# Seven products in place of eight for the output projection of a bilinear feed-forward block, with tokens split by parity

## The chip, the cores and the metric

The kernel runs on one core of a Trainium2 chip. The metric is device time in microseconds (us), the median of several executions; a change counts as faster or slower from 2% on. Ratios are the mean time of one kernel's fast runs over that of the other's fast runs in the same rounds, so they differ a little from the ratio of the medians quoted.

Engines in the profile's lines: PE is TensorE's matmul, PEld its weight load, DVE VectorE, ACT ScalarE, POOL GpSimd, SP SyncE.

## The reference

```python
# attention: batch 8, heads 8, seq 576, head_dim 64; 4 heads local (32 back), 4 strided (every 32nd)
scores = q @ k.T / 8, masked;  attn = softmax(scores);  x = attn @ v      # -> x: 4608 tokens x 512
a = x @ w_a                       # 512 -> 1536
b = x @ w_b                       # 512 -> 1536
out = (a * b) @ w_out             # 1536 -> 512
```

The change concerns the last line alone.

## The kernel before: the parts concerned

Tokens go in nine tiles of 512. A tile has twelve *blocks* of d_ff: eight matmuls of 512 columns give 128 rows of a and of b in PSUM (call the twelve together the *wide part*). ScalarE copies a to SBUF, and VectorE multiplies it by b into `pf`. Four groups of twelve matmuls then make the output (the *output stretch*). A tile is 16 slots; between slots, score units (S) and value units (V) of the next batch's attention are put in.

```python
def ffn_ab(t, f, mid, ab=None):
    ...
    ab = [psum4["mm"].tile([128, TTOK], F32, tag="mm", name="mm") for _ in range(2)]   # 3 banks in all
    ...                                              # 4 + 4 matmuls of 512 columns
    nc.scalar.copy(a_sb, ab[0])
    nc.vector.tensor_mul(pf[:, f, :], a_sb, ab[1])   # 512 bf16, one plain run

def ffn_y(t, j, mid):
    ...
    for f in range(FD):                              # 12
        nc.tensor.matmul(y, lhsT=pf[:, f, 128 * j:128 * (j + 1)], rhs=wo_sb[:, f, c0:c0 + n], ...)
    ...                                              # copy to SBUF, store

def step_VT(b, u):                                   # value unit: 6 or 8 matmuls, then
    ...
    nc.scalar.activation(r, sums, ACT.Ln)
    nc.scalar.activation(r, r, ACT.Exp, scale=-1.0)
    ...                                              # two VectorE multiplications that wait for these
```

In the traces VectorE takes its instructions in program order (the prediction shows it idle for 2.61 us with ready work behind).

The softmax here doesn't subtract the row's maximum and nothing guards it: scores larger than these inputs give would overflow.

## Time and profile before

| | before |
|---|---|
| time, median (lowest to highest) | 343.75 us (342.25 to 344.11) |
| TensorE busy | 98% |
| VectorE, ScalarE busy | 60%, 60% |
| wide part of tile 4, its output stretch | 24.05 us, 11.40 us |
| wide part of tile 7 (no attention), its output stretch | 20.72 us, 10.36 us |

The last two rows are stretches from the first matmul of one part to the first of the next. The lines behind them are in the prediction.

### The profile page before, as it was taken

How to read it: one execution, taken by the hardware profiler on the slowest of the kernel's cores; microseconds unless marked ns; L12 is line 12 of the kernel's file. 1: busy time of each engine (PE TensorE's matmuls, PEld its weight loads, DVE VectorE, ACT ScalarE, POOL GpSimd, SP SyncE). 2: the span in 40 equal slices, each digit the busy share in tenths (PEclk: the TensorE clock that was granted, in tenths of full speed). 3: DMA queues.
4: the chain of work that ended last, by engine and by line, in shares of the span. 5: the costliest groups of instructions: out<-in, count | busy, mean ns of one | idle time of the engine just before them, and what ended most of it. 6: DMA issues, size and time to landing. Idle time of an engine off the chain costs nothing.

```text
span 341.5 us, 6887 instructions
## 1 busy us (share of the span) xinstructions
PE 333.1 (98%) x2520; PEld 173.7 (51%) x2520; DVE 205.1 (60%) x400; ACT 203.9 (60%) x331; POOL 140.4 (41%) x247
## 2 busy tenths in 40 slices
PE   8999999989989999999999999999999999999995
PEld 6754555445545555555555555555555444444444
DVE  6866657758759766876578846885666333303331
ACT  5754865368767765876587657775688533223311
POOL 8945539898537434653465346633000000000000
PEclk9999999999999999999999999999999999999999
DMA  9999999997999599969997989888220110021002
GB/s 160 154 203 197 202 176 172 179 154 89 129 200 101 90 99 185 99 110 91 165 104 133 77 168 96 132 80 145 76 59 2 61 63 0 0 92 34 0 31 94
DMA packets 102242, 37.56 MB, mean 110 GB/s; under 512 B 77632, under 2 KB 97728, under 8 KB 102208
## 3 DMA queue, kind: packets, MB, share of 16 engines
q0 software_dynamic: 87760, 19.58, 63.7%
q1 hardware_dynamic: 14304, 17.47, 16.2%
q8 instruction: 20, 0.33, 0.4%
q14 instruction: 14, 0.11, 0.1%
q10 hardware_dynamic: 144, 0.07, 0.1%
HBM read 39.71 MB, written 9.44 MB: 144 GB/s over the span
## 4 chain that ended last, share of the span: by engine, by line
PE 70%; DMA 17%; SPq 3%; DVE 3%; ACT 3%; POOL 2%; issue 2%; DVEq 0%; ACTq 0%
PE mm L518 41%; PE mm L546 20%; DMA vl<-in_v_dram 4%; PE o L438 3%; PE st L340 3%; DMA k<-in_k_dram 3%; DMA wa_sb<-in_moe_w_a_dram 3%; SPq L302 2%; DMA qz01l<-tq 2%; PE misc L153 2%; DMA out_dram<-y_sb 1%; DMA qz01s<-tq 1%; ACT xr L447 1%; DMA qz11s<-tq 1%; DVE tq L283 1%
## 5 line engine op out<-in xcount | busy, mean ns | idle before, releaser
L518 PE MATMUL mm<-xT,wb_sb 128*128 128x512 bf16 x424 | 110.1, 379 | 0.3
L518 PE MATMUL mm<-xT,wa_sb 128*128 128x512 bf16 x424 | 110.2, 379 | 0.1
L536 DVE TENSOR_TENSOR pf<-a_sb,mm 128x512 bf16<-128x512 f32 x106 | 71.9, 678 | 48.3 <-PE mm L518 25.5
L546 PE MATMUL mm<-wo_sb,pf 128*128 128x512 bf16 (+2 forms) x456 | 99.6, 368 | 0.1
L535 ACT COPY a_sb<-mm 128x512 f32<-128x512 f32 x106 | 62.1, 586 | 45.4 <-PE mm L518 43.0
L518 PEld LDWEIGHTS <-wb_sb 128*128 128x128 bf16 x432 | 41.7, 98 | 49.5 <-issue 1.3
L546 PEld LDWEIGHTS <-pf 128*128 128x128 bf16 x456 | 41.5, 98 | 42.3 <-issue 0.4
L518 PEld LDWEIGHTS <-wa_sb 128*128 128x128 bf16 x432 | 38.1, 98 | 34.2 <-issue 0.2
L552 ACT COPY y_sb<-mm 128x512 f32<-128x512 f32 (+2 forms) x35 | 20.0, 571 | 46.6 <-PE mm L546 38.6
L348 ACT ACTIVATE p<-st 128x576 bf16<-128x576 f32 (+1 forms) x64 | 41.7, 651 | 8.8 <-PE st L340 8.2
L447 ACT ACTIVATE xr<-o 64x576 f32<-64x576 f32 x48 | 31.1, 647 | 23.5 <-PE o L438 23.3
L454 DVE TENSOR_TENSOR xT<-o,xr 64x288 bf16<-64x288 f32 x48 | 21.6, 450 | 33.1 <-ACT xr L448 32.8
L448 ACT ACTIVATE xr<-xr 64x576 f32<-64x576 f32 x48 | 32.8, 682 | 1.5
L452 DVE TENSOR_TENSOR xT<-o,xr 64x288 bf16<-64x288 f32 x48 | 21.6, 450 | 16.9 <-ACT xr L448 16.4
L678 POOL CAST pace<-pf 1x1 f32<-1x1 bf16 x51 | 11.6, 227 | 41.5 <-DVE pf L536 41.3
L358 DVE TENSOR_TENSOR p<-p,mask_l 128x576 int16<-128x576 int16 x32 | 14.6, 455 | 17.1 <-ACT p L348 17.1
L218 POOL DMA_DIRECT2D vs<-in_v_dram x24 | 19.6, 817 | 9.9 <-issue 9.9
L194 POOL DMA_DIRECT2D kl<-in_k_dram x24 | 16.0, 666 | 6.7 <-issue 5.0
L194 POOL DMA_DIRECT2D ql<-in_q_dram x24 | 16.0, 666 | 6.6 <-DMA wo_sb<-in_moe_w_out_dram 3.8
L185 POOL DMA_DIRECT2D natk<-in_k_dram x24 | 14.6, 610 | 3.6 <-issue 3.0
L185 POOL DMA_DIRECT2D natq<-in_q_dram x24 | 14.6, 609 | 0.0
L678 POOL COPY pace<-y_sb 1x1 f32<-1x1 f32 x22 | 4.2, 189 | 24.2 <-ACT y_sb L552 24.2
(116 smaller groups left out, 316.2 us busy)
## 6 DMA issues: line engine op xcount, KB each, us to landing
out_dram<-y_sb SPq DMA_DIRECT2D x35, 256.0 KB, 2.4
vl<-in_v_dram POOLq DMA_DIRECT2D x7, 384.0 KB, 6.6
kl<-in_k_dram POOLq DMA_DIRECT2D x24, 72.0 KB, 2.8
ql<-in_q_dram POOLq DMA_DIRECT2D x24, 72.0 KB, 3.3
vs<-in_v_dram POOLq DMA_DIRECT2D x24, 72.0 KB, 3.6
wo_sb<-in_moe_w_out_dram POOLq DMA_DIRECT2D x4, 384.0 KB, 11.9
natk<-in_k_dram POOLq DMA_DIRECT2D x20, 72.0 KB, 3.3
natq<-in_q_dram POOLq DMA_DIRECT2D x20, 72.0 KB, 3.3
```

The costliest lines, as they stand in the source:

```text
L185: nc.gpsimd.dma_start(out=t[32 * h:32 * h + n], in_=bass.AP(tensor=src.tensor, offset=(b * H + HL + h) * S * D, ap=[[RS * D, n], [YS * RS ...
L194: nc.gpsimd.dma_start(out=t[32 * h:32 * h + 32], in_=src[b, h].rearrange("(i y) d -> y i d", y=32))
L348: nc.scalar.activation(p[:M, :, :W], st[:M, :, :W], ACT.Exp, scale=scale)
L447: nc.scalar.activation(r, sums, ACT.Ln)
L448: nc.scalar.activation(r, r, ACT.Exp, scale=-1.0)
L452: nc.vector.tensor_mul(dst[:, W * half:W * (half + 1)], o[:64, j, :W], r[:, j])
L454: nc.vector.tensor_mul(dst.rearrange("d (p r) -> d p r", r=RS)[:, :, G * half:G * (half + 1)], o[:64, j, :W].rearrange("d (g p) -> d p g", ...
L518: nc.tensor.matmul(ps_, lhsT=w[:, kk, 128 * f:128 * (f + 1)], rhs=xT[:, kk, TTOK * t:TTOK * (t + 1)], start=(kk == first), stop=(kk == last))
L535: nc.scalar.copy(a_sb, ab[0])
L536: nc.vector.tensor_mul(pf[:, f, :], a_sb, ab[1])
L546: nc.tensor.matmul(y, lhsT=pf[:, f, 128 * j:128 * (j + 1)], rhs=wo_sb[:, f, c0:c0 + n], start=(f == 0), stop=(f == FD - 1))
L552: (nc.scalar.copy if act else nc.vector.tensor_copy)(y_sb, y)
```

## The change

Strassen's scheme makes a product of 2 x 2 blocks from seven block products. The blocks here are: tokens even and odd, d_ff blocks even and odd, output columns left and right. Seven products of half the columns replace eight, so TensorE should gain an eighth of the output product in tiles 1 to 8. For it, sums of the blocks of `pf` (VectorE and GpSimd) and of `w_out` (VectorE, once) are needed, and the products are combined afterwards. To make room in SBUF, x is kept for four batches in a ring, and the sums of `pf` share a buffer with the loads of the first batches.

```diff
+    XR = 4
-    xT = const.tile([128, KD, n_tok], BF16)
+    xT = const.tile([128, KD, XR * S], BF16)          # a tile across the ring's end: two matmuls for one
 ...
+        if t in FAST_Y:                                # tiles 1 to 8
+            halves = lambda x: x.rearrange("p (m i) -> p m i", i=2)
+            nc.vector.tensor_mul(pf[:, f, :].rearrange("p (i m) -> p m i", i=2), halves(a_sb), halves(ab[1]))
+        else:
             nc.vector.tensor_mul(pf[:, f, :], a_sb, ab[1])
 ...
+    def fast_s(t, n, gs):                              # sums of blocks: n = 0 on GpSimd, 1 and 2 on VectorE
 ...
+            if k == "3":   v["a"] = copy of bank a     # ScalarE
+            elif k == "4": v["w"] = bank b + v["a"]    # VectorE
+            elif k == "1": v["e"] = bank c + v["w"]    # VectorE
+            elif k == "2": v["y21"] = copy of bank b; v["h"] = v["w"] - v["y21"]   # ScalarE, GpSimd
+            elif k == "5": v["y12"] = copy of bank a; v["g"] = v["e"] - v["y12"]   # ScalarE, GpSimd
+            elif k == "6": v["y22"] = bank c + v["h"]  # VectorE
+            else:          v["y11"] = v["g"] - bank d  # VectorE
 ...
+        # products 3, 4, 1 open banks a, b, c; 2, 5, 6 are added onto b, a, c; 7 opens d
+        for k, b, lhs, rhs in (("3", "a", ...), ("4", "b", ...), ("1", "c", ...),
+                               ("2", "b", ...), ("5", "a", ...), ("6", "c", ...), ("7", "d", ...)):
+            ...                                        # 2 x 6 matmuls of 256 columns each
```

(The code of the combining is shortened to one line per product.) The banks also rotate over four in place of three from tile 1 on. The two lines with `halves` put even tokens into the first half of the row and odd ones into the second; in the order in which the program lists the elements, element 0 goes to place 0, element 1 to place 256, element 2 to place 1, and so on. The output rows are stored by parity accordingly.

More of the change, by code (lines that the diff above doesn't have):

```diff
@@ L26 @@
 WCH = (0, 2, 5, 8, 10, 12)
+FAST_Y = (1, 2, 3, 4, 5, 6, 7, 8)
 @with_exitstack
@@ L160, with fast_w @@
     wo_sb = wp.tile([128, FD, d_model], BF16)
+    FG = FD // 2
+    HT = TTOK // 2
+    HN = d_model // 2
+    wf = wp.tile([128, 5, FG, HN], BF16, name="wf")
+    wov = wo_sb.rearrange("p (g e) (j n) -> p e j g n", e=2, j=2)
+    def fast_w(n, gs):
+        a, b, op = ((wov[:, 0, 1], wov[:, 1, 1], ALU.subtract), (wov[:, 1, 0], wov[:, 0, 0], ALU.subtract),
+                    (wov[:, 0, 0], wov[:, 1, 1], ALU.add), (wov[:, 0, 0], wov[:, 0, 1], ALU.add),
+                    (wov[:, 1, 0], wov[:, 1, 1], ALU.add))[n]
+        nc.vector.tensor_tensor(wf[:, n, gs], a[:, gs], b[:, gs], op=op)
     tl = {}
@@ L168 @@
     nats = {}
+    shared = {}
     def load_qk(b, strided, heads=range(HL), names="kq"):
@@ L174, in load_qk @@
                 n, R, h0 = (NP, RS, HL) if strided else (96, RL, 0)
-                if (b, nm, strided) not in nats:
-                    nats[b, nm, strided] = nat.tile([n, HL, R, D], BF16, tag=f"{nm}{R}", name=f"{nm}{R}", bufs=1)
-                t = nats[b, nm, strided]
+                w0 = {"k6": 0, "q6": 1536, "k8": 3072, "q8": 5120}[f"{nm}{R}"]
+                if b not in shared:
+                    shared[b] = nat.tile([128, 5 * FD * TTOK // 4], BF16, tag="shared", name="shared")
+                t = nats[b, nm, strided] = shared[b][:n, w0:w0 + HL * R * D].rearrange("p (h r d) -> p h r d", r=R, d=D)
                 hs = slice(heads[0], heads[-1] + 1)
@@ L449, in step_VT @@
         for j in range(2):
-            dst = xT[64 * j:64 * j + 64, c, S * b:S * (b + 1)]
+            dst = xT[64 * j:64 * j + 64, c, S * (b % XR):S * (b % XR + 1)]
             if c < 2:
@@ L469, in X_e @@
         tv = tp.rearrange("d (g p) -> d g p", p=n)
-        dst = xT[:, c, S * b:S * (b + 1)]
+        dst = xT[:, c, S * (b % XR):S * (b % XR + 1)]
         if c >= 2:
@@ L511, with mm_bank @@
     pfs = {}
+    used = [0]
+    def mm_bank(shape):
+        nm = "tp" if used[0] % 4 == 3 and used[0] >= 0 else "mm"
+        used[0] += 1
+        return psum4[nm].tile(shape, F32, tag=nm, name="mm")
     def ab_mm(t, f, ab, kks, mid=None, first=0, last=KD - 1):
+        n = min(TTOK, XR * S - TTOK * t % (XR * S))
+        cuts = [(0, n)] + ([(n, TTOK - n)] if n < TTOK else [])
         for w, ps_ in zip((wa_sb, wb_sb), ab):
@@ L517, in ab_mm @@
             for kk in kks:
-                nc.tensor.matmul(ps_, lhsT=w[:, kk, 128 * f:128 * (f + 1)], rhs=xT[:, kk, TTOK * t:TTOK * (t + 1)],
-                                 start=(kk == first), stop=(kk == last))
+                for c0, n in cuts:
+                    x0 = (TTOK * t + c0) % (XR * S)
+                    nc.tensor.matmul(ps_[:, c0:c0 + n], lhsT=w[:, kk, 128 * f:128 * (f + 1)], rhs=xT[:, kk, x0:x0 + n],
+                                     start=(kk == first and c0 == 0), stop=(kk == last and c0 == cuts[-1][0]))
     def ffn_ab(t, f, mid, ab=None):
@@ L525, in ffn_ab @@
         if ab is None:
-            ab = [psum4["mm"].tile([128, TTOK], F32, tag="mm", name="mm") for _ in range(2)]
+            ab = [mm_bank([128, TTOK]) for _ in range(2)]
             if f == 0:
@@ L535, in ffn_ab @@
         nc.scalar.copy(a_sb, ab[0])
-        nc.vector.tensor_mul(pf[:, f, :], a_sb, ab[1])
-        return pf[:1, f, :1]
+        if t in FAST_Y:
+            halves = lambda x: x.rearrange("p (m i) -> p m i", i=2)
+            nc.vector.tensor_mul(pf[:, f, :].rearrange("p (i m) -> p m i", i=2), halves(a_sb), halves(ab[1]))
+        else:
+            nc.vector.tensor_mul(pf[:, f, :], a_sb, ab[1])
+        return pf[:1, f, :1]
+    pss = {}
+    def fast_s(t, n, gs):
+        if t not in pss:
+            pss[t] = nat.tile([128, 5 * FD * TTOK // 4], BF16, tag="shared", name="ps").rearrange("p (g m) -> p g m", g=FG)
+        s = pss[t][:, gs]
+        x = pfs[t].rearrange("p (g e) (i m) -> p g e i m", e=2, i=2)[:, gs]
+        if n == 0:
+            nc.gpsimd.tensor_tensor(s[:, :, 0:HT], x[:, :, 0, 0], x[:, :, 1, 1], op=ALU.add)
+        elif n == 1:
+            nc.vector.tensor_tensor(s[:, :, HT:3 * HT].rearrange("p g (i m) -> p g i m", i=2), x[:, :, 0], x[:, :, 1], op=ALU.add)
+        else:
+            nc.vector.tensor_tensor(s[:, :, 3 * HT:].rearrange("p g (e m) -> p g e m", e=2), x[:, :, :, 1], x[:, :, :, 0],
+                                    op=ALU.subtract)
@@ new lines, with y_plan, f32t, store @@
+    yst = {}
+    def y_plan(t):
+        pf, s = pfs[t], pss[t]
+        full = lambda e, i: (lambda g, q: pf[:, 2 * g + e, HT * i + 128 * q:HT * i + 128 * (q + 1)])
+        summed = lambda n: (lambda g, q: s[:, g, HT * n + 128 * q:HT * n + 128 * (q + 1)])
+        wsum = lambda n: (lambda g: wf[:, n, g])
+        wfull = lambda e, j: (lambda g: wov[:, e, j, g])
+        bank = {}
+        v = {}
+        def f32t(nm, bufs):
+            return fsb.tile([128, 2, HN], F32, tag=nm, name=nm, bufs=bufs)
+        def store(y, i, j, q=slice(0, 2), n=slice(0, HN)):
+            rows = out[TTOK * t:TTOK * (t + 1), HN * j:HN * (j + 1)].rearrange("(q p i) c -> p i q c", q=2, i=2)
+            nc.sync.dma_start(out=rows[:, i, q, n], in_=y[:, q, n])
+        def post(k):
+            if k == "3":
+                v["a"] = f32t("ya", 1)
+                nc.scalar.copy(v["a"], bank["a"])
+            elif k == "4":
+                v["w"] = v["a"]
+                nc.vector.tensor_tensor(v["w"], bank["b"], v["a"], op=ALU.add)
+            elif k == "1":
+                v["e"] = f32t("ye", 1)
+                nc.vector.tensor_tensor(v["e"], bank["c"], v["w"], op=ALU.add)
+            elif k == "2":
+                v["y21"] = f32t("y_sb", 4)
+                nc.scalar.copy(v["y21"], bank["b"])
+                store(v["y21"], 1, 0)
+                v["h"] = v["w"]
+                nc.gpsimd.tensor_tensor(v["h"], v["w"], v["y21"], op=ALU.subtract)
+            elif k == "5":
+                v["y12"] = f32t("y_sb", 4)
+                nc.scalar.copy(v["y12"], bank["a"])
+                store(v["y12"], 0, 1)
+                v["g"] = v["e"]
+                nc.gpsimd.tensor_tensor(v["g"], v["e"], v["y12"], op=ALU.subtract)
+            elif k == "6":
+                v["y22"] = f32t("y_sb", 4)
+                nc.vector.tensor_tensor(v["y22"], bank["c"], v["h"], op=ALU.add)
+                store(v["y22"], 1, 1)
+            else:
+                last(slice(0, 2), slice(0, HN))
+        def last(q, n):
+            if "y11" not in v:
+                v["y11"] = f32t("y_sb", 4)
+            nc.vector.tensor_tensor(v["y11"][:, q, n], v["g"][:, q, n], bank["d"][:, q, n], op=ALU.subtract)
+            store(v["y11"], 0, 0, q, n)
+        for k, b, lhs, rhs in (("3", "a", full(0, 0), wsum(0)), ("4", "b", full(1, 1), wsum(1)), ("1", "c", summed(0), wsum(2)),
+                               ("2", "b", summed(2), wfull(0, 0)), ("5", "a", summed(1), wfull(1, 1)),
+                               ("6", "c", summed(3), wsum(3)), ("7", "d", summed(4), wsum(4))):
+            new = b not in bank
+            if new:
+                bank[b] = mm_bank([128, 2, HN])
+            tail = k == "7" and t == NT - 1
+            for q in range(2):
+                for n in ((slice(0, 128), slice(128, 256)) if tail and q == 1 else (slice(0, HN),)):
+                    for g in range(FG):
+                        nc.tensor.matmul(bank[b][:, q, n], lhsT=lhs(g, q), rhs=rhs(g)[:, n],
+                                         start=new and q == 0 and g == 0, stop=g == FG - 1, skip_group_check=True)
+                        if g == FG - 1:
+                            if tail:
+                                last(slice(q, q + 1), n)
+                            elif q == 1:
+                                post(k)
+                        yield v
@@ L539, in ffn_y, with ffn_ys @@
+    def ffn_ys(t, j, mid):
+        if j == 0:
+            yst[t] = y_plan(t)
+        n = 21 + (6 if (t, j) == (NT - 1, 3) else 0)
+        for i in range(n):
+            v = next(yst[t])
+            if i == n // 2:
+                mid()
+        if j == 3:
+            for _ in yst[t]:
+                pass
+        return v[("a", "e", "y12", "y11")[j]][:1, 0, :1]
     def ffn_y(t, j, mid):
@@ L543, in ffn_y @@
         for z, n in enumerate((256, 128, 128) if (t, j) == (NT - 1, 3) else (d_model,)):
-            y = psum4["mm"].tile([128, n], F32, tag="mm", name="mm")
+            y = mm_bank([128, n])
             for f in range(FD):
@@ L549, in ffn_y @@
                     mid()
-            y_sb = fsb.tile([128, n], F32, tag="y_sb", name="y_sb", bufs=3)
+            y_sb = fsb.tile([128, n], F32, tag="y_sb", name="y_sb", bufs=4)
             act = t < NT - 1 or (j + z) % 2 == 1
@@ L631 @@
         for t in range(NT):
-            slots += [(ffn_ab, t, f) for f in range(FD)] + [(ffn_y, t, j) for j in range(4)]
+            slots += [(ffn_ab, t, f) for f in range(FD)] + [(ffn_ys if t in FAST_Y else ffn_y, t, j) for j in range(4)]
         steps = {}
@@ L672 @@
             do(i, fill_v, t)
+        for n in range(5):
+            for z in range(2):
+                do(17 + 2 * n + z, fast_w, n, slice(3 * z, 3 * z + 3))
+        for t in FAST_Y:
+            for n, at_ in ((0, (3, 7, 11)), (1, (4, 8, 11)), (2, (5, 9, 11))):
+                for z in range(3):
+                    do(16 * t + at_[z], fast_s, t, n, slice(2 * z, 2 * z + 2))
         for i, (fn, t, j) in enumerate(slots):
+            if i == 0:
+                used[0] = -1000 * 3
+            elif i == 16:
+                used[0] = 0
             mid = lambda: take(i - 0.5)
-            done = fn(t, j, mid) if fn is ffn_y else fn(t, j, mid, first.get(j) if t == 0 else None)
+            done = fn(t, j, mid) if fn is not ffn_ab else fn(t, j, mid, first.get(j) if t == 0 else None)
             if i > 13 and i in at:
```

## The prediction

> **What bounds the kernel now.** I read the page's busy shares first, then sums by stretch, then the timelines of TensorE and VectorE around one output product.
>
> ```profile
> span 341.5 us, 6887 instructions
> PE 333.1 (98%) x2520; PEld 173.7 (51%) x2520; DVE 205.1 (60%) x400; ACT 203.9 (60%) x331; POOL 140.4 (41%) x247
> ```
>
> TensorE is busy for 98%. A busy row alone could be padding, since the page says that ends are modelled, so I looked at starts. The timeline of the last tile has groups of four matmuls of 512 columns:
>
> ```profile
> 317.97 1.03 PE L518 MATMUL mm<-xT,wb_sb 128*128 128x512 bf16 x4
> 318.84 1.03 PE L518 MATMUL mm<-xT,wa_sb 128*128 128x512 bf16 x4
> 319.70 1.03 PE L518 MATMUL mm<-xT,wb_sb 128*128 128x512 bf16 x4
> ```
>
> A group starts every 0.865 us: 216 ns a matmul, not the 379 ns of the rows. TensorE really streams. Sums by stretch, columns as on the page (stretch, length, then PE, PEld, DVE, ACT, POOL busy, clock, DMA):
>
> ```profile
> 170.07:194.12 24.05, 24.02 (x185) 12.52 (x183) 18.22 (x34) 19.09 (x31) 13.00 (x26) 1.00 0.96 105
> 194.12:205.52 11.40, 11.40 (x83) 5.72 (x80) 6.58 (x13) 5.82 (x11) 5.01 (x10) 1.00 0.84 148
> 296.39:306.75 10.36, 10.36 (x49) 4.70 (x48) 0.69 (x1) 1.76 (x3) 0.00 (x0) 1.00 0.20 76
> 335.25:336.56 1.31, 1.31 (x14) 1.17 (x13) 0.69 (x1) 0.00 (x0) 0.00 (x0) 1.00 0.05 13
> ```
>
> The first two are tile 4: its two wide products, then its output product with two value and two score units in it. The third is tile 7's output product alone, 48 matmuls: 10.36/48 = 216 ns. The fourth runs from the first of the twelve 256-column matmuls of the tail to the matmul after them: 1.31/12 = 109 ns. So half the columns cost half the time, and the separate weight load of each, although its row says 98 ns, stays hidden. The only long TensorE waits are some 3 us around 68 and 94 us, for transposed q landing. **TensorE's stream is the bound, in every tile.**
>
> VectorE is at 18.22 of 24.05 us in the wide part, and does its work strictly in program order. Its timeline at tile 4's output product, which starts at 194.12 (I call that T):
>
> ```profile
> 194.67 0.69 DVE L536 TENSOR_TENSOR pf<-a_sb,mm 128x512 bf16<-128x512 f32 x1
> 195.28 0.45 DVE L358 TENSOR_TENSOR p<-p,mask_s 72x576 int16<-72x576 int16 x1
> 195.65 0.70 DVE L288 STREAM_TRANSPOSE tk<-natk 128x512 bf16<-128x512 bf16 x1
> 198.96 0.91 DVE L454 TENSOR_TENSOR xT<-o,xr 64x288 bf16<-64x288 f32 x2 [2.61 <-ACT xr L448]
> 199.91 1.46 DVE L288 STREAM_TRANSPOSE tk<-natk 128x512 bf16<-128x512 bf16 x2
> ```
>
> To be seen here: VectorE stands idle 2.61 us for ScalarE's logarithm and exponential of value unit 6, while two transposes whose data has long landed wait behind it. Whatever is queued behind that unit waits too. Today nothing that TensorE needs is behind it.
>
> [...]
>
> ```profile
> L358 DVE TENSOR_TENSOR p<-p,mask_l 128x576 int16<-128x576 int16 x32 | 14.6, 455 | 17.1 <-ACT p L348 17.1
> L536 DVE TENSOR_TENSOR pf<-a_sb,mm 128x512 bf16<-128x512 f32 x106 | 71.9, 678 | 48.3 <-PE mm L518 25.5 <-ACT a_sb L535 21.2
> ```
>
> 576 16-bit elements take 455 ns, 512 fp32 ones 678 ns. [...]
>
> **The change, part by part.**
>
> *Taken from TensorE.* A tile's output product was 48 x 216 = 10.36 us. It becomes 7 products x 2 token halves x 6 blocks = 84 matmuls of 256 columns, 84 x 109.2 = 9.17 us: 1.19 us less, 9.5 us over eight tiles. The attention matmuls are unchanged. All of this lies on the path.
>
> *Given back by the ring.* 4 x 576 = 2304 tokens are 4.5 tiles, so tile 4's inputs wrap: 96 matmuls of 512 become 192 of 256, 96 x (2 x 109.2 - 215.9) = +0.24 us. The overwritten batches were read over a tile earlier: no wait. Batch 1's loads wait for all transposes of batch 0, but they were issued at 15 us, after the last of those (12.7 us): nothing.
>
> *Added to VectorE, per tile.* Six bf16 sums of 1024 elements[...], about 0.69 us each, 4.1 us; four fp32 combinations of 512 at 0.69 us, 2.8 us. Together 6.9 us in 35.5 us, of which some 25 are busy and several more are in-order waits. The ten weight sums, once, in tile 1: 768 elements, about 0.55 us, 5.5 us.
>
> *ScalarE* loses one copy of 0.59 us per tile. *GpSimd* gets five adds[...] in a tile where it has room (some 18 of 35.5 us used), but in order behind its DMA issues of 0.7 to 1.5 us.
>
> *The new wait.* Order of products: 3, 4, 1, 2, 5, 6, 7. Product 2 is added onto product 4's bank and must wait until VectorE has read that one ("4" + "3"). In program order that read stands behind unit 6 and the transpose of that slot. With tile 4's own durations, from T:
> - products 3 and 4 up to the 21st matmul: 21 x 0.109 = 2.29. There unit 6's eight matmuls go in (0.26). Product 4 ends at 2.88, product 1 could end at 4.19.
> - Unit 6's multiplications follow its matmuls' start by 1.86 us where ScalarE is free (for the unit before it: 191.87 to 193.73), so they begin at 2.29 + 1.86 = 4.15. VectorE has by then done the mul of block 11, mask, transpose and the two new sums (0.55 + 0.61 + 0.37 + 0.70 + 2 x 0.61 = 3.45), so they don't push it.
> - Two multiplications 0.95, transpose 0.71: the read starts at 5.81 and ends at 6.50; product 2 starts near 6.6 instead of 4.19. **TensorE stands 2.4 us.**
> - Inside that, GpSimd's last sum for product 1 stands behind a DMA issue that ended at 3.36 after T[...].
> - Afterwards product 6's bank (read right after) and the next tile's banks come free before they are wanted: no second wait.
>
> Sum for tiles 2 to 5: -1.19 + 2.4 = +1.2 each. Tile 6 has no transposes: read 5.06 to 5.75, stall 1.7, net +0.5. Tiles 7 and 8 have no attention, VectorE is idle: the full -1.19 each. The last tile's product 7 is read in pieces from the bank that is still written, where the baseline used separate banks: +0.8, estimated from two reads of 0.3 to 0.4. Tile 1: the units sit elsewhere, but the read stands behind a mask, a unit and a transpose: about 2.2 of stall, +0.7 for VectorE crowded by the weight sums, and about 1.2 of the present wait for q near 94 us overlaps the new wait: -1.19 + 2.2 + 0.7 - 1.2 = +0.5.
>
> Total: +0.5 (tile 1) + 4 x 1.2 + 0.5 - 2.4 + 0.24 + 0.8 = +4.4, or 348.2; I shade it to 347.5, because a placement carried through eight tiles may hide more than I see.
>
> **The rivals.** (a) No stall: product 2 finds its bank read. Then 343.75 - 9.5 + 0.24 = 334.5, or 2.7% faster. For it: the four-bank rotation and the spread of the sums show care, and VectorE is only 60% busy. Against it: the 2.61 us idle row with ready work behind it. (b) VectorE itself becomes the bound: 25 + 6.9 us plus waits for ScalarE of about 0.7 us per value unit make 36 to 38 us, above the tile's present 35.5. Then the wide part also waits for banks, and tiles 1 to 5 cost 1 to 2 us more each: 353 to 356. Against it: four banks instead of three give each block 0.86 us more, and the stall lets VectorE catch up. (c) GpSimd is slower than estimated[...]: product 1 then sets the stall, some tenths more per tile, 349.
>
> **Range and chances.** The saving of 9.3 is firm; the stalls, about 13, are uncertain by some 5 (six tiles, 0.8 each, together). Low end 340 (stalls halved), high end 353 (rival b in part). Faster by 2% needs under 336.9, so stalls under 2.5 us in all: 0.14. Slower by 2% needs above 350.6: 0.20. Within: 0.66.
>
> **What would show it.** Right: in tiles 2 to 5 a gap of about 2.4 us before the 37th matmul of the output product, released by VectorE's add on the bank; the add right behind a transpose and the multiplications of unit 6; output stretch 12.6 us against 11.40; tile 7's stretch 9.2 against 10.36; the wide part of tile 4 at 24.0 to 24.5. Wrong: output stretches near 10.2 us (rival a), wide parts over 25 us (rival b), or a gap before the 29th matmul released by GpSimd that is the longer one (rival c). A VectorE sum of more than 0.8 us, or a strided write of the products that takes more than 678 ns, would also break my sizes.

The sum came to +4.4 us, or 348.2, recorded as 347.5. The 0.69 us for a block sum and 0.55 for a weight sum (in the 6.9 and 5.5 us, and so in rival (b)) stay as estimates, since rows of the kernel before lead to them: 288 fp32 elements take 450 ns (the multiplications of L454) and 512 take 678, about 1 ns an element; 576 16-bit ones take 455, much as 288 fp32 ones do. So 1024 16-bit elements come to about 0.68 us and 768 to 0.55. That product 2 starts only after the whole read of its bank was an assumption when this was written; the halves kernel below fits it (the read ends 6.38 us into the stretch, product 2 starts at 6.44).

## More of the kernel before

In tile 7, where VectorE does nothing but the product, its timeline in the kernel before is this (start, length, engine, line, operation, then in brackets how long the engine was idle and what ended it):

```profile
284.58 0.69 DVE L536 TENSOR_TENSOR pf<-a_sb,mm 128x512 bf16<-128x512 f32 x1 [1.04 <-PE mm L518]
286.30 0.69 DVE L536 TENSOR_TENSOR pf<-a_sb,mm 128x512 bf16<-128x512 f32 x1 [1.04 <-PE mm L518]
```

One product every 1.72 us, which is eight matmuls of TensorE, and VectorE waits 1.04 us for each.

## The result, and the profile after

| | before | after |
|---|---|---|
| time, median | 343.93 us | 479.28 us (478.21 to 479.54) |
| ratio | | 1.3925 (95% interval 1.387 to 1.398) |
| VectorE busy | 205.1 us, 60% | 418.3 us, 88% |
| wide part of tile 4, its output stretch | 24.05, 11.40 us | 37.12, 17.38 us |
| wide part of tile 7, its output stretch | 20.72, 10.36 us | 27.82, 12.50 us |

The result is correct, and 39% slower (the median of before is now that of four runs, one more than above). The page of the changed kernel, with its row for the product (busy us, mean ns of one, then the idle time before), and two lines of its list of waits (us in total, times, longest):

```profile
PE 355.8 (74%) x2855; PEld 214.3 (45%) x2886; DVE 418.3 (88%) x489; ACT 201.2 (42%) x324; POOL 199.6 (42%) x314
...
DVE 43%; issue 19%; PE 19%; DMA 11%; ACT 3%; POOL 3%; DVEq 0%; POOLq 0%; SPq 0%; ACTq 0%
...
L565 DVE TENSOR_TENSOR pf<-a_sb,mm 128x512 bf16<-128x512 f32 x96 | 229.0, 2441 | 5.3 <-ACT a_sb L562 4.7
...
PE mm L545 <- DVE pf L565: 64.6, 64, 2.9
ACT a_sb L562 <- DVE pf L565: 98.4, 75, 3.3
```

The second line is the chain that ended last by engine: VectorE leads it, where TensorE had 70% before. The third says why. The product, 678 ns before with the same shape and types, takes 2441 ns. That is 1.763 us more, 96 times: 169 us of VectorE's work. TensorE and ScalarE now wait for it; the waits on bank reads that the prediction was about come far behind. Sums by stretch (columns as in the prediction) for the wide part of tile 4, its output stretch and the wide part of tile 7:

```profile
233.88:271.00 37.12, 25.66 (x281) 21.82 (x278) 36.90 (x39) 18.82 (x30) 15.99 (x30) 1.00 0.66 75
271.00:288.38 17.38, 13.70 (x119) 10.31 (x117) 13.64 (x19) 5.63 (x10) 8.16 (x13) 0.80 0.52 83
392.27:420.09 27.82, 22.05 (x96) 9.33 (x96) 26.18 (x16) 7.04 (x12) 4.38 (x9) 1.00 0.07 25
```

In the wide part of tile 4 VectorE is busy 36.90 of 37.12 us. TensorE's granted clock is lower in this kernel (0.951 in the mean, against 0.998), but that is not the cause: the wide parts of tiles 3 and 5 take 36.84 us each, at clocks of 0.95 and 1.00. It may count a little in the output stretches: tile 4's took 17.38 us at 0.80, tile 3's 16.54 us at 1.00. Tile 7 shows a full VectorE (26.18 of 27.82 us) without any attention; its timeline:

```profile
396.65 9.46 DVE L565 TENSOR_TENSOR pf<-a_sb,mm 128x512 bf16<-128x512 f32 x4
...
399.34 1.02 PE L545 MATMUL mm<-xT,wb_sb 128*128 128x512 bf16 x4 [0.38 <-DVE pf L565]
...
399.37 0.59 ACT L562 COPY a_sb<-mm 128x512 f32<-128x512 f32 x1 [1.68 <-DVE pf L565]
```

Beside the timeline of before: four products follow each other without a gap in 9.46 us, one every 2.27 us or so, where TensorE could bring one every 1.72 us. It is now TensorE that waits (0.38 us, for a bank) and ScalarE (1.68 us, for a free copy buffer). The order of who waits for whom has turned round.

### The profile page after: what moved, and what is told of

It is laid out like the page before. It is cut to its first block, busy times and chain, and to the rows that moved or that the text cites. A ratio compares the mean times of both kernels' runs of the same rounds, so it can differ in the third digit from the quotient of the medians.

```text
span 477.7 us, 7736 instructions
## 1 busy us (share of the span) xinstructions
PE 355.8 (74%) x2855; PEld 214.3 (45%) x2886; DVE 418.3 (88%) x489; ACT 201.2 (42%) x324; POOL 199.6 (42%) x314
## 4 chain that ended last, share of the span: by engine, by line
DVE 43%; issue 19%; PE 19%; DMA 11%; ACT 3%; POOL 3%; DVEq 0%; POOLq 0%; SPq 0%; ACTq 0%
DVE pf L565 24%; PE mm L649 10%; PE mm L545 6%; DVE p L374 3%; DMA vl<-in_v_dram 3%; DVE xT L468 3%; PE o L454 2%; DVE xT L470 2%; DMA shared<-in_k_dram 2%; DMA wa_sb<-in_moe_w_a_dram 2%; DVE ps L582 2%; DVE tq L304 1%; DVE tq L299 1%; DVE ps L580 1%; DVE tk L299 1%
## 5 line engine op out<-in xcount | busy, mean ns | idle before, releaser
L565 DVE TENSOR_TENSOR pf<-a_sb,mm 128x512 bf16<-128x512 f32 x96 | 229.0, 2441 | 5.3 <-ACT a_sb L562 4.7
L545 PE MATMUL mm<-xT,wb_sb 128*128 128x512 bf16 (+1 forms) x465 | 111.6, 363 | 64.2 <-DVE pf L565 63.7
L545 PE MATMUL mm<-xT,wa_sb 128*128 128x512 bf16 (+1 forms) x451 | 111.3, 366 | 2.2 <-DVE pf L565 0.9
L649 PEld LDWEIGHTS <-ps 128*128 128x128 bf16 x486 | 47.7, 102 | 20.6 <-POOL ps L578 9.2
L463 ACT ACTIVATE xr<-o 64x576 f32<-64x576 f32 x48 | 31.1, 647 | 49.5 <-PE o L454 49.4
L649 PE MATMUL mm<-wf,pf 128*128 128x256 bf16 x192 | 31.1, 307 | 24.6 <-DVE pf L565 24.5
L649 PE MATMUL mm<-wf,ps 128*128 128x256 bf16 (+1 forms) x294 | 40.1, 285 | 7.3 <-POOL ps L578 6.4
L649 PEld LDWEIGHTS <-pf 128*128 128x128 bf16 x192 | 18.4, 107 | 33.1 <-DVE pf L565 29.6
L578 POOL TENSOR_TENSOR ps<-pf 128x512 bf16<-128x512 bf16 x24 | 28.2, 1176 | 0.2
L649 PE MATMUL mm<-wo_sb,ps 128*128 128x256 bf16 x192 | 24.8, 282 | 2.1 <-DVE ya L610 1.9
L582 DVE TENSOR_TENSOR ps<-pf 128x1024 bf16<-128x1024 bf16 x24 | 19.1, 794 | 0.0
L580 DVE TENSOR_TENSOR ps<-pf 128x1024 bf16<-128x1024 bf16 x24 | 18.1, 756 | 0.4
```

The costliest lines, as they stand in the source:

```text
L545: nc.tensor.matmul(ps_[:, c0:c0 + n], lhsT=w[:, kk, 128 * f:128 * (f + 1)], rhs=xT[:, kk, x0:x0 + n], start=(kk == first and c0 == 0), sto ...
L565: nc.vector.tensor_mul(pf[:, f, :].rearrange("p (i m) -> p m i", i=2), halves(a_sb), halves(ab[1]))
L578: nc.gpsimd.tensor_tensor(s[:, :, 0:HT], x[:, :, 0, 0], x[:, :, 1, 1], op=ALU.add)
L582: nc.vector.tensor_tensor(s[:, :, 3 * HT:].rearrange("p g (e m) -> p g e m", e=2), x[:, :, :, 1], x[:, :, :, 0], op=ALU.subtract)
L649: nc.tensor.matmul(bank[b][:, q, n], lhsT=lhs(g, q), rhs=rhs(g)[:, n], start=new and q == 0 and g == 0, stop=g == FG - 1, skip_group_check ...
```

## The experiments

### Which side of the product is slow, and what the rest of the change is worth

Theory A: the write, which jumps by 256 elements (512 B) each time, costs the 1.76 us. Theory B: the order of the operands or PSUM does. Theory C: the waits that the prediction worked out make the change slow, and VectorE is full on top, so that the time stays above 370 us even with a fast product.

The first kernel swaps the sides: the same values at the same places, but the write is in one run and the reads have a step of two.

```diff
-            halves = lambda x: x.rearrange("p (m i) -> p m i", i=2)
+            halves = lambda x: x.rearrange("p (m i) -> p i m", i=2)
-            nc.vector.tensor_mul(pf[:, f, :].rearrange("p (i m) -> p m i", i=2), halves(a_sb), halves(ab[1]))
+            nc.vector.tensor_mul(pf[:, f, :].rearrange("p (i m) -> p i m", i=2), halves(a_sb), halves(ab[1]))
```

> The changed kernel with the parity split on the reading side: the product is written in one run of 512 bf16 elements, and the two fp32 operands are read with step two; values and places are the same, so the result is right. Theory A (the write that jumps 512 B with every 2-byte element costs the 1.76 us): the product falls from 2.44 us to 0.68 to 0.8 us, VectorE from 418 us busy to about 255, and the time to what the prediction on record foresaw, 340 to 353 us. Theory B (the operand order or the PSUM read costs it): the product stays above 1.5 us and the time above 400 us. Theory C (the change is slow for its waits on product 4's bank, and VectorE would be full anyhow): time above 370 us with a fast product.

Measured: 353.93 us (ratio 1.0262, interval 1.022 to 1.0305), correct. The product's row in its page:

```profile
L565 DVE TENSOR_TENSOR pf<-a_sb,mm 128x512 bf16<-128x512 f32 x96 | 64.9, 676 | 23.4 <-PE mm L545 18.1
```

676 ns, as before the change. One edit of an order of letters gives back 125.4 of the 135.4 us; VectorE's busy time falls to 262.9 us. Theory B falls, and so does C as the cause of the 135 us: some 10 us over the kernel before are left for the waits. The time lies just above the band of 340 to 353 us.

The second kernel has no reordering at all: the tile's first and second 256 tokens take the place of even and odd ones.

```diff
-            halves = ...
-            nc.vector.tensor_mul(pf[:, f, :].rearrange("p (i m) -> p m i", i=2), halves(a_sb), halves(ab[1]))
+            nc.vector.tensor_mul(pf[:, f, :], a_sb, ab[1])
 ...
-            rows = out[...].rearrange("(q p i) c -> p i q c", q=2, i=2)
+            rows = out[...].rearrange("(i q p) c -> p i q c", q=2, i=2)
```

> The changed kernel with tokens split into halves of the tile in place of parities: the product is plain on both sides, and the output rows are stored accordingly; the result is right. Theory A: product 0.68 us, time 340 to 353 us, equal to the read-side run within 1%; if step-two reads cost something, this run is the faster of the two. In it the wait before product 2 shows without VectorE being full: about 2.4 us in tiles 2 to 5. Theory C: above 370 us.

Measured: 352.99 us (ratio 1.0244, 1.0206 to 1.0282), correct, product 676 ns. Within 0.3% of the first: reads of fp32 with step two cost nothing that shows here (676 ns a product in both), and neither does storing the rows by parity. This kernel, which I call *halves*, is the base of what follows.

The third kernel puts the write alone into the kernel before.

```diff
-        nc.vector.tensor_mul(pf[:, f, :], a_sb, ab[1])
+        if t > 0:
+            halves = lambda x: x.rearrange("p (m i) -> p m i", i=2)
+            nc.vector.tensor_mul(pf[:, f, :].rearrange("p (i m) -> p m i", i=2), halves(a_sb), halves(ab[1]))
+        else: ...
 ...                                                   # rows stored accordingly
```

> The kernel before with nothing but the parity write of the product in tiles 1 to 8 (the output product reads the blocks where they now lie, the rows are stored accordingly; right result). Theory A: the product takes 2.4 us here too; VectorE gets 12 x 1.75 = 21 us more per tile, so the attention tiles grow from 35.5 to some 45 to 48 us, tiles 7 and 8 (12 x 2.3 = 28 us against 31 us of TensorE) hardly: 400 to 430 us in all. If the write were only slow for what else the change does (GpSimd's adds, the sums), it would take 0.7 us here and the time stay at 344.

Measured: 436.86 us in its one run, correct; 92.6 us over the median of the kernel before. Its row for the product, and the sums for the wide part of tile 4:

```profile
L538 DVE TENSOR_TENSOR pf<-a_sb,mm 128x512 bf16<-128x512 f32 x96 | 227.8, 2431 | 17.6 <-ACT a_sb L535 16.1
```
```profile
210.56:247.71 37.15, 26.73 (x180) 13.53 (x182) 35.62 (x34) 19.93 (x32) 12.04 (x24) 0.95 0.63 70
```

So nothing else of the change is needed for the slow product, and it alone costs 92.6 of the 135.4 us. The wide part of tile 4 is as long as in the changed kernel (37.15 against 37.12 us); the rest lies mostly in tile 1 and in the output stretches (12.23 against 17.38 us in tile 4). In those of the changed kernel TensorE waits 24.5 us in all for late products. My size was too small: tile 4 takes 49.4 us in all, not 45 to 48, and the wide part of tile 7 27.53 instead of 20.72, since there too VectorE's row of twelve products is longer than TensorE's wide part. I had compared it with the whole tile of TensorE, but the products can't spread over the output stretch, which needs all of them.

### What in a write is slow

The fourth kernel is the kernel before with fourteen probes behind its end, four of each. Its time as a whole says nothing, and its output is right.

```diff
+        for _ in range(4):
+            mul(pw, pa, pp)                                                             # probe 1, line 693
+        for _ in range(4):                                                              # probe 2, line 695
+            mul(r2(pw, "p (i m) -> p m i", i=2), r2(pa, "p (m i) -> p m i", i=2), r2(pp, "p (m i) -> p m i", i=2))
+        ...                                                                             # probe n, line 691 + 2 n
```

> The kernel before with probes behind its end, four of each on otherwise idle engines, each with a line of its own: the product of two fp32 tiles written (1) plainly, (2) as in the change, (3) written plainly but read with step two, (4) written with step two, (5) as in the change but into fp32, (6) as in the change with both operands in SBUF, (7) alternating between the two halves in runs of 2, (8) of 8 and (9) of 32 elements, (10) alternating between places 16 B apart, (11) alternating between places 8 B apart, (12) written with a step of 16 B in one long run; then a copy on VectorE (13) and one on ScalarE (14) with the write of the change. Theory A1 (a write is slow when it enters another 16-byte line with every element): 2, 5, 6, 10 and 12 slow (2.4 us), 1, 3, 4, 8, 9 and 11 at 0.68, 7 between. Theory A2 (an inner run of two elements is slow as such): 2, 5, 6, 7, 10 and 11 slow, 12 fast. Theory B (the read): 3 slow too. The time of the whole says nothing.

The groups of its probes (busy us, mean ns of one, idle):

```profile
L719 ACT CAST pr_w<-pr_a 128x512 bf16<-128x512 f32 x4 | 9.8, 2445 | 70.6 <-DVE pr_w L717 70.5
L711 DVE TENSOR_TENSOR pr_w<-pr_a,pr_p 128x512 bf16<-128x512 f32 x4 | 9.7, 2422 | 0.1
L715 DVE TENSOR_TENSOR pr_w<-pr_a,pr_p 128x512 bf16<-128x512 f32 x4 | 9.7, 2418 | 0.1
...
L695 DVE TENSOR_TENSOR pr_w<-pr_a,pr_p 128x512 bf16<-128x512 f32 x4 | 9.6, 2408 | 0.1
L717 DVE CAST pr_w<-pr_a 128x512 bf16<-128x512 f32 x4 | 5.8, 1456 | 0.1
L701 DVE TENSOR_TENSOR pr_v<-pr_a,pr_p 128x512 f32<-128x512 f32 x4 | 4.1, 1037 | 0.1
L699 DVE TENSOR_TENSOR pr_w<-pr_a,pr_p 128x512 bf16<-128x512 f32 x4 | 2.9, 724 | 0.1
L705 DVE TENSOR_TENSOR pr_w<-pr_a,pr_p 128x512 bf16<-128x512 f32 x4 | 2.8, 689 | 0.1
...
L713 DVE TENSOR_TENSOR pr_w<-pr_a,pr_p 128x512 bf16<-128x512 f32 x4 | 2.7, 687 | 0.1
...
L693 DVE TENSOR_TENSOR pr_w<-pr_a,pr_p 128x512 bf16<-128x512 f32 x4 | 2.7, 687 | 0.2
```

| write | probe | ns |
|---|---|---|
| plain | 1 | 687 |
| as in the change | 2 | 2408 |
| plain, read with step two | 3 | 688 |
| step of 2 elements (4 B) | 4 | 724 |
| as in the change, into fp32 | 5 | 1037 |
| as in the change, both operands in SBUF | 6 | 2417 |
| alternating in runs of 2, 8, 32 elements | 7, 8, 9 | 689, 687, 688 |
| alternating between places 16 B apart | 10 | 2422 |
| alternating between places 8 B apart | 11 | 687 |
| step of 8 elements (16 B), inner run of 64 | 12 | 2418 |
| as in the change, copy on VectorE; on ScalarE | 13; 14 | 1456; 2445 |

Theory A1 holds for the bf16 products tried: slow (2408 to 2422 ns a product, against 687 to 724) are exactly those writes in which each 2-byte element goes into another 16 bytes than the one before it. The distance beyond that does not matter (2422 and 2418 ns at 16 B, 2408 at 512 B). The length of the inner run doesn't either, which was A2: probe 11 has inner runs of two and is fast (687 ns), probe 12 has long ones and is slow (2418 ns). Two elements per visit are enough (probe 7, 689 ns; I had expected something between). It is no matter of PSUM (probe 6, 2417 ns) nor of the read (probe 3, 688 ns). ScalarE's copy with this write is slow too: 2445 ns, against 586 for its plain copy of this size into fp32 and 651 for an activation that writes 576 bf16 elements plainly, both elsewhere in the kernel. What I had wrong: the fp32 write of probe 5 is slowed to 1037 ns only (0.7 ns more an element, against 3.4 for bf16). Why 2-byte elements cost so much more, and why the copy takes 1456, these runs don't tell.

### The waits that the prediction had worked out

With the product at its old speed, the halves kernel shows the part of the prediction that the slow write had covered. Output stretch of tile 4, from 201.78 us on: VectorE, then GpSimd, then TensorE.

```profile
205.93 0.92 DVE L470 TENSOR_TENSOR xT<-o,xr 64x288 bf16<-64x288 f32 x2 [0.41 <-ACT xr L464]
206.88 0.71 DVE L304 STREAM_TRANSPOSE tk<-natk 128x512 bf16<-128x512 bf16 x1
207.51 0.65 DVE L609 TENSOR_TENSOR ya<-mm,ya 128x512 f32<-128x512 f32 x1
```
```profile
204.61 0.81 POOL L234 DMA_DIRECT2D vs<-in_v_dram  x1 [0.84 <-issue]
205.44 1.16 POOL L577 TENSOR_TENSOR ps<-pf 128x512 bf16<-128x512 bf16 x1
```
```profile
206.66 1.05 PE L648 MATMUL mm<-wf,ps 128*128 128x256 bf16 x8 [1.39 <-POOL ps L577]
208.22 2.02 PE L648 MATMUL mm<-wo_sb,ps 128*128 128x256 bf16 x17 [0.51 <-DVE ya L609]
```

The value unit's multiplications begin 4.15 us after the stretch's start (predicted 4.15), then the transpose, then the read of product 4's bank, which ends at 6.38 (predicted 6.50). Product 2 starts at 6.44 (predicted 6.6; without a wait 4.19). GpSimd's sum stands behind the DMA issue (it starts at 205.44 us, when the issue of 204.61 us has taken its 0.81), and product 1 waits for it on the way: that is the longer of the two gaps, 1.39 against 0.51 us. The whole stretch is 12.67 us, predicted 12.6. Of the 12.67, some 0.22 us are no wait: the record of the next tile's first matmul is missing from the trace (the last score matmul starts at 214.19 us, the first recorded matmul of tile 5 at 214.45), so 12.45 is nearer. Tenths of a microsecond in these stretches are not resolved.

The next kernels take these waits away. First the order of the products: 7, which opens a bank of its own, goes third, and 5 before 2; GpSimd's sum goes ahead of the issue in its slot. For product 7 VectorE's two sums change places too.

```diff
+        if t < NT - 1:
+            plan = [plan[i] for i in (0, 1, 6, 2, 4, 3, 5)]        # 3 4 7 1 5 2 6
+        for k, b, lhs, rhs in plan:
 ...
-            else:
+            if k == ("2" if t < NT - 1 else "7"):                 # y11, once g is there
                 last(slice(0, 2), slice(0, HN))
 ...                                                              # placed ahead of the DMA issues of a slot:
+            for n, at_ in ((0, (3, 7, 11)), (2, (5, 9, 11)), (1, (4, 8, 11))):
```

> The kernel with token halves, and the products of tiles 1 to 7 in the order 3, 4, 7, 1, 5, 2, 6 (product 7, which needs no bank read, comes before the two that did wait); GpSimd's last sum for product 1 goes ahead of that slot's DMA issue. Theory D (the 2.2 us per tile are the wait of product 1 for GpSimd's sum and of product 2 for the read of its bank, nothing else): the output stretch of tiles 2 to 5 falls from 12.67 to 10.3 to 10.7 us, that of tile 6 from 11.34 to about 10.0, tile 1 gains 1 to 2 us; the whole loses 9 to 12 us against the halves kernel (352.99), so 341 to 344. Rival E (VectorE is too full in program order, and the wait only moves, to product 6 or to the next tile's banks): the stretch or the wide part after it keeps at least half of the 2.2 us, 347 to 352 in all.

Measured: 343.91 us (ratio 0.9973, 0.9923 to 1.0024: the same as before), correct. The output stretches of tiles 2 to 5 are 10.21 us each, of tile 6 9.70: the old 11.40 and 10.89 less 1.19, which is the whole of the gain worked out. Theory D holds there; the two waits went together, so their shares were not tested apart. But the wide parts grew (tile 4: 24.25 to 25.57 us), so E holds in part: half of the wait of tile 4 came back later. Tile 1 gained next to nothing: its output stretch fell from 17.82 to 15.95 us, its wide part grew from 25.85 to 27.55.

Then tile 1, where the prediction's +0.5 us was far off: in the halves kernel its output stretch is 17.82 us against 14.04 before.

```diff
-FAST_Y = (1, 2, 3, 4, 5, 6, 7, 8)
+FAST_Y = (2, 3, 4, 5, 6, 7, 8)
-                do(17 + 2 * n + z, fast_w, n, slice(3 * z, 3 * z + 3))
+                do(17 + 4 * n + 2 * z, fast_w, n, slice(3 * z, 3 * z + 3))
```

> The kernel with token halves, but tile 1 with the plain output product, and the ten weight sums spread over the 20 slots of tile 1 and the start of tile 2. Theory F (tile 1 alone lost some 4 us because weight sums and product sums fill VectorE there): tile 1's output stretch returns from 17.82 to 14 to 14.5 us, tiles 2 to 5 keep their 12.6, the whole falls by 3 to 4 us against 352.99: 349 to 350. Rival: tile 1's 17.82 came from the transfers of q that tile 1 waited for before; then less than 1.5 us is gained.

Measured: 347.72 us (ratio 1.0069, 1.0011 to 1.0127: the same as before), correct; tile 1's stretch 14.51 us. Tiles 3 and 5 keep 12.45 and 12.56 us; tiles 2 and 4 took 14.11 each, at a granted clock of 0.88 in the profiled run, the slowest of the five. The gain, 5.3 us, is more than I expected, and the rival falls. Theory F holds for the larger part: in the halves kernel's output stretch of tile 1 TensorE waits 1.92 and 1.05 us for late products on VectorE. It also waits 2.22 us there for GpSimd's sum, as in the other tiles, and the edit takes that away too. In the halves kernel one can see a second piece of the crowding, VectorE and GpSimd in one another's way, in tile 1:

```profile
86.07 1.63 DVE L581 TENSOR_TENSOR ps<-pf 128x1024 bf16<-128x1024 bf16 x1
```
```profile
85.77 1.39 POOL L577 TENSOR_TENSOR ps<-pf 128x512 bf16<-128x512 bf16 x1
```

The sum that takes a median of 0.68 us elsewhere takes 1.63 us when it starts 0.30 us after a GpSimd add: it ends 0.54 us after that one has ended, as if it had begun about there. GpSimd's add took 1.39 us there, against 1.17 in the mean. It is no single case. In the timelines of the halves kernel from 60 to 106 us and from 201 to 214 us, 6 VectorE operations with both operands in SBUF overlap a GpSimd addition or subtraction by more than 0.15 us, and all 6 are lengthened, by 0.34 to 1.15 us (a mask of 0.45 us to 1.60). The four others that overlap one by as much are not: a transpose takes 0.77 us, three pairs of multiplications with an operand in PSUM 0.91 or 0.92, as where no add runs. All 6 are also 16-bit, so the two properties are not told apart.

Both edits together, and separate banks for the pieces of the last product:

```diff
+        def part(q, n):                                            # last tile, second half: two free banks
+            ...
+            ends[0] = psum4["o"].tile([128, 2, 512], F32, tag="o", name="o")
```

> Both edits, and the last tile's product 7 in separate banks for its pieces. If both theories hold: seven tiles at 1.19 us less than before, 0.24 for the tile that the ring cuts, some 0.5 for the weight sums: 336 to 339.5 us, 1.4 to 2.4% faster than the kernel before (344.25). Under rival E: 344 to 348.

Measured: 339.06 us (ratio 0.9845, 0.98 to 0.9889), correct: within what was expected, and ahead of the kernel before, but at 2% unclear. The output stretches of tiles 2 to 5 are 10.21 us again, the last tile's, to the end of its matmuls, 10.04 after 10.72. The wide parts of tiles 3 to 5 are still 24.86 to 25.30 us, about 1 us over those of before. A gap of 0.5 us from start to start (idle 0.35 to 0.38) some 3.4 us into them waits for VectorE's read of product 6's bank, which itself waits for a GpSimd subtraction. So the last kernel regroups the sums: VectorE reads each bank at once, and GpSimd subtracts afterwards.

```diff
             elif k == "1":
                 v["e"] = bank c + v["w"]
+                v["y11"] = v["e"] - bank d                         # VectorE, at once
 ...
             elif k == "6":
-                v["y22"] = bank c + v["h"]
+                v["y22"] = bank c + v["w"]                         # VectorE, at once
+                v["y22"] -= v["y21"]                               # GpSimd
```

> The kernel of both edits, with the sums of tiles 2 to 7 regrouped so that no read of a bank waits for GpSimd: VectorE takes product 7 from the sum right after product 1, and product 6 plus the sum right after product 6; GpSimd's subtractions come afterwards, in SBUF. Theory G (of the 0.8 to 1.3 us per tile that the wide parts of tiles 3 to 5 gained against the kernel before, half is the wait of the next tile's second block for the bank of product 6, the rest late transposes of q): the 0.5 us gap early in the wide part goes, VectorE waits less, the wide parts of tiles 3 to 5 fall from 24.9-25.3 to 24.1-24.6 us; the whole 336 to 338.5. Rival: the wide parts stay, as the late q is what counts and it follows from VectorE's load: 338.5 to 340.

Measured: 336.08 us (335.75 to 336.87; ratio 0.9764, interval 0.9735 to 0.9793), correct: faster. Theory G's time holds: the wide parts of tiles 3 to 5 are back at 23.91, 24.11 and 24.30 us, so nearly all of the 0.8 to 1.3 us came back. The 0.5 us gap is gone, and a wait of more than 0.3 us for late q transposes is left in one of these tiles (0.32 us), where two had one (0.44 and 0.62). That suggests that the reads that waited for GpSimd had held back the transposes too; it was not tested apart. Tile 4 of this kernel, its wide part and its output stretch, columns as above:

```profile
167.90:192.01 24.11, 24.11 (x281) 21.86 (x278) 21.20 (x40) 18.63 (x30) 18.31 (x30) 1.00 1.06 137
192.01:202.22 10.21, 10.21 (x119) 9.24 (x116) 9.66 (x19) 5.67 (x10) 7.95 (x12) 1.00 0.77 97
```

TensorE is busy for 24.11 of 24.11 and 10.21 of 10.21 us, beside a VectorE at 21.20 of 24.11 us. This is the fastest kernel here, 2.4% ahead of the kernel before.

## Why the prediction was wrong, point by point

**The step that failed** is "Added to VectorE, per tile": its list of six sums and four combinations (6.9 us) leaves out the product that was there already. The terms that are listed were right (a block sum took 0.65 to 0.68 us in the halves kernel where no GpSimd add overlapped it). I left the product at 678 ns since its shape and types are the same, and named the strided write only at the end as something that "would also break my sizes". It measured 2441 ns: 12 x 1.763 = 21.2 us more per tile, three times all that I had counted. That makes VectorE and not TensorE's stream the bound: VectorE was busy for 36.90 of the 37.12 us of tile 4's wide part. So rival (b), VectorE as the bound, is what happened, but at 479 us and not the 353 to 356 that the sum without this term gave; and the argument against it (a fourth bank, a stall to catch up in) bore on a lack of tenths, not of ten microseconds. Probe 2 and the first kernel measure the term, the third shows that the write alone is enough for it and costs 92.6 of the 135.4 us.

**TensorE's saving** was right: 1.19 us per output stretch, seen as 11.40 to 10.21 us once nothing waits, and 10.36 to 9.17 in tile 7 of the last kernel (9.27 in the halves kernel).

**The new wait** was right in its end and its sum, as the halves kernel shows: product 2 starts 6.44 us into the stretch, against 6.6, and the stretch is 12.67 (12.45) us against 12.6. How it shows was wrong. I had named as the sign one gap of about 2.4 us before the 37th matmul; there it was 0.51. The longer gap, 1.39 us, is before the 29th and ended by GpSimd, which I had put down as the sign of rival (c). My own working had such a gap inside the wait (in a clause that is cut, as it rested on a time for GpSimd's add that no trace showed), and I left it out of the signs. The reason given for (c), a GpSimd slower than estimated, can't be judged without that estimate; the trace shows an add of 1.16 us that stood behind the DMA issue.

**Tile 1** was wrong by itself: +0.5 us predicted, 3.8 us in the output stretch of the halves kernel. The stall of 2.2 us was about right in size (2.22 us for GpSimd's sum and 0.21 for the bank), but I took 0.7 for VectorE's crowding, where TensorE waited 1.92 and 1.05 us for late products: about 5.5 us of weight sums and 4.1 us of block sums met a VectorE that already had few gaps there. This, with half a microsecond more at the tail than the 0.8 I gave it (waits of 0.73 and 0.54 us there), is most of what separates the halves kernel's 353.0 from my 347.5.

**The ring** did what was said: tile 4's wide part in the halves kernel is 24.25 us against 24.05.

**Two sums** of the prediction don't quite close, without consequence: tile 6's read would begin at 4.15 + 0.95 = 5.10, not 5.06, and rival (b), 1 to 2 us in each of five tiles, adds 5 to 10 us, more than its band of 353 to 356 spans.

## What to carry to other kernels

An operation that a change only gives another access pattern is a changed operation: cost the write by how many elements in a row fall into the same 16 bytes (for a bf16 product of 512, one: 2408 ns, two: 689), and put a reordering on the side that reads, or choose the split so that none is needed. What was free here is an fp32 read with a step of two (688 ns, against 687); wider steps of a read were not tried. Where an engine works in program order, as VectorE did here, a short read that frees a bank costs what stands in front of it in the queue (in the halves kernel TensorE went on from product 4 at 2.89 us into the stretch, and the read of its bank, 0.65 us long, ended at 6.38); move it, or the work that waits for it, rather than make it faster. When a first, large error is found, take it out and look again: here the remaining 9 us, of which the prediction had explained nearly half, became a gain of 8 us by following its own chain.
